# Chunked attention followed by a top-2 expert layer on one Trainium2 core: constants issued ahead of the loads, logits and rank products one iteration later, block-diagonal V and memory rows, selection by counting, and the spill one-hot in a pool of its own

## The chip, the cores and the metric

The kernel runs on one core of a Trainium2 chip. A core has five engines with a queue of instructions each: TensorE (PE, and PEld for its weight loads), VectorE (DVE), ScalarE (ACT), GpSimd (POOL) and SyncE (SP). The last two also issue DMA transfers here, as does ACT. The metric is the device time of one execution in microseconds (us), lower is better.

## What is computed

The reference has two stages. Attention works on chunks of 32 queries, each of which sees 16 keys to the left, its own 32, 8 to the right, and 8 memory keys (64 columns in all). Its output, 3072 rows of 512, goes through a router that picks two of eight experts for each row.

```python
# q, k, v: (4, 8, 768, 64); mem_k, mem_v: (4, 8, 8, 64); chunk, left, right = 32, 16, 8
for c in range(S // chunk):
    k_full = concat([mem_k, k[max(0, 32*c-16) : min(S, 32*c+40)]])
    v_full = concat([mem_v, v[...same rows...]])
    a = softmax(q[32*c : 32*c+32] @ k_full.T / 8)
    out[32*c : 32*c+32] = a @ v_full
x = out.transpose(0, 2, 1, 3).reshape(3072, 512)

noisy = x @ w_gate + log1p(exp(x @ w_noise)) * noise      # (3072, 8)
top2 = two largest of noisy per row;  w = softmax over those two
for e in range(8):
    for each row with e among its two:
        out[row] += w[row, e] * (relu(x[row] @ w1[e]) @ w2[e])   # w1 512x1024, w2 1024x512
```

## The kernel before

**Attention, 16 iterations.** The 32 heads are taken two at a time; such a pair fills the 128 partitions (head 0 on 0 to 63, head 1 on 64 to 127). Two pairs make a group, so there are eight groups of loads. All loads of Q, K, V and expert weights are issued by POOL in program order, which also issues the gathers and scatters later. `qg`, `kg` and `vg` have three buffers each; before the loop POOL issues groups 0, 1 and 2, and in the loop group `i // 2 + 2` at every even `i`.

The loop at L456 is a software pipeline, written out by hand; the order in the code is the order on every engine. Iteration `i` emits:

- `PT_pe(i-1)`: six PE transposes of the softmax numerators `P` into `p_p` (L259)
- `max_dve(i)`: DVE row maximum of the scores (L245)
- `qkT_pe(i+2)`: 24 PE transposes of Q and K into `p_t` (L212), with four ACT copies out of PSUM (L214)
- `PT_dve(i-1)`: DVE copy of `p_p` to `PT` (L264)
- `sub_dve(i)`: DVE subtraction of the maximum (L250) and ACT exponential to `P` (L252)
- `PV_pe(i-1)`: `PT` times memory rows and V into `ps_o` (L275, L281)
- `scores_pe(i+1)`: 116 small PE products into `ps_s`, of which there is one buffer (L224 to L237)
- `mult_dve(i-1)`: DVE reciprocal and scaling of `ps_o` into `xrow` (L292, L293)
- `xT_pe(i-2)`: six PE transposes of `xrow` into `p_x` (L301), and an ACT copy to `xt` (L303)
- `logits_pe(i-2)`: six PE products of `xt` with the gate and noise weights into `ps_l` (L311)

The PSUM tiles `p_p`, `p_t`, `p_x`, `ps_r` and `ps_t` share three buffers.

**Routing.** After every fourth pair a batch of 768 rows has its logits, and `route(b)` gives nine closures: `s1` (ACT softplus, DVE noisy logits `nl`), `s2` and `s3` (two rounds of maximum, comparison, code and maximum on DVE for the two experts `e1`, `e2`; from these the two-hot `two` and the pair one-hot `oh`; then PE rank products `ps_r`, L366 to L371), `s4` (gate weights, and an SP DMA of the rows to `x_rows`), `s4b` and `s5` (DVE token codes, ranks, and six one-hots `Rn`), `s6` (PE table `ps_t`, L407), `s7`, `s8` (DVE table `tab` and counts `seen`). The loop runs `s1` in the iteration that emits the batch's last logits and takes three closures from the list at the end of each iteration.

**Between the stages.** From the table the kernel forms the gather indices `gidx`, and from rows that overflow a bucket a spill list: `ov`, PE counts `ps_v`, the one-hot `sone` (DVE, L530), and its products `ps_w` (PE, L535). `sone` is in the pool `ap`, whose memory is given free after that; the gather buffers `xl` are laid over it.

**Experts.** POOL gathers 28 buckets of 128 rows by index (L572), PE transposes them (L581), and for eight experts PE does `ps_h` (L636) and `ps_y` (L644); DVE sums, POOL scatters (L652).

## Time and profile before

| | |
|---|---|
| median of 3 runs (lowest to highest) | 413.27 us (412.27 to 416.29) |
| the profiled execution: its time | 414.79 us |
| its span, first to last instruction | 413.1 us |
| PE busy | 307.4 us (74%), 4522 matmul instructions |
| DVE / ACT / POOL busy | 164.1 / 119.4 / 124.2 us |
| mean granted TensorE clock | 0.835 of 2.4 GHz |
| DMA | 42.98 MB, mean 104 GB/s |

The profile is one execution on the chip. A slice is a fortieth of the span, 10.3 us; slices 0 to 15 hold attention, and the experts' first product starts at 175.43 us. A matmul's recorded time includes its latency, so groups of matmuls are read from start to start.

### The profile page before, as it was taken

The numbers are of one execution on the slowest core, as the hardware profiler recorded it, in microseconds if no ns is written. First come the engines' busy times: TensorE is split into PE (matmuls) and PEld (weight loads), VectorE is DVE, ScalarE is ACT, GpSimd is POOL, SyncE is SP. The second block draws the span as 40 slices with busy tenths as digits, with TensorE's granted clock in tenths as the row PEclk, the third lists the DMA queues.
The fourth block names the chain that finished last, engine by engine and source line by source line (L and its number), as shares of the span: only waits on it lengthen the run. The fifth ranks groups of instructions, "written<-read, shape, count | busy, mean of one in ns | idle before, by whom it ended". The sixth has DMA issues, their size and how long they took to land.

```text
span 413.1 us, 10205 instructions
## 1 busy us (share of the span) xinstructions
PE 307.4 (74%) x4522; PEld 189.5 (46%) x4540; DVE 164.1 (40%) x377; ACT 119.4 (29%) x235; POOL 124.2 (30%) x141
## 2 busy tenths in 40 slices
PE   0045863766577462387899899899998999999990
PEld 0034652545456352264447447445454454554540
DVE  0005554745765776433214223233334242443440
ACT  1035643336335222022233233223130321312200
POOL 8840531315160000476110051060242403123061
PEclk9998585558556555578999999999999999999996
DMA  9999799699499520169960049068095852712021
GB/s 100 168 160 103 51 119 125 104 124 76 113 143 210 140 64 21 41 109 198 196 116 2 2 82 198 2 127 163 33 177 128 143 116 86 120 46 89 2 109 55
DMA packets 83327, 42.98 MB, mean 104 GB/s; under 512 B 57255, under 2 KB 76711, under 8 KB 83280
## 3 DMA queue, kind: packets, MB, share of 16 engines
q0 software_dynamic: 74928, 38.85, 65.1%
q1 hardware_dynamic: 8064, 3.38, 3.0%
q8 instruction: 37, 0.61, 0.6%
q10 hardware_dynamic: 288, 0.07, 0.1%
q14 instruction: 10, 0.08, 0.1%
HBM read 61.32 MB, written 10.65 MB: 174 GB/s over the span
## 4 chain that ended last, share of the span: by engine, by line
PE 65%; DVE 10%; issue 10%; ACT 5%; DMA 5%; POOL 3%; POOLq 0%; DVEq 0%; ACTq 0%
PE ps_h L636 23%; PE ps_y L644 20%; PE p_t L212 5%; DMA vg<-in_v_dram 4%; ACT xt L303 3%; PE p_x L301 2%; PE ps_o L281 2%; PE p_t L581 2%; PE p_p L259 2%; PE ps_o L275 2%; PE ps_s L234 2%; ACT qT L214 2%; POOL out_dram L652 2%; DVE xTb L582 1%; PE ps_l L311 1%
## 5 line engine op out<-in xcount | busy, mean ns | idle before, releaser
L636 PE MATMUL ps_h<-xTb,w1t 128*128 128x512 bf16 (+3 forms) x608 | 109.4, 330 | 1.1 <-DVE xTb L582 1.0
L644 PE MATMUL ps_y<-w2t,ht 128*128 128x512 bf16 x430 | 98.9, 379 | 1.0 <-issue 0.2
L636 PEld LDWEIGHTS <-w1t 128*128 128x128 bf16 x864 | 65.2, 99 | 46.0 <-issue 2.8
L624 DVE TENSOR_SCALAR ht<-ps_h 128x416 bf16<-128x416 f32 (+2 forms) x68 | 41.7, 613 | 82.9 <-PE ps_h L636 80.9
L652 POOL DMA_INDIRECT out_dram<-acc,sidx x28 | 28.0, 999 | 144.9 <-DVE acc L651 142.4
L644 PEld LDWEIGHTS <-ht 128*128 128x128 bf16 x448 | 42.3, 98 | 48.9
L622 ACT ACTIVATE ht<-ps_h 128x416 bf16<-128x416 f32 (+2 forms) x68 | 36.4, 535 | 80.8 <-PE ps_h L636 75.6
L117 POOL DMA_DIRECT2D vg<-in_v_dram x34 | 33.0, 975 | 61.0 <-PE ps_o L281 58.3
L572 POOL DMA_INDIRECT xl<-x_rows,gidx x28 | 29.2, 1041 | 68.2 <-DVE ov1b L515 46.6
L636 PE MATMUL ps_h<-xTs,w1t 128*128 128x32 bf16 x256 | 45.9, 179 | 0.2 <-issue 0.2
L648 ACT ACTIVATE acc<-ps_y,meta 128x512 f32<-128x512 f32 x28 | 19.2, 687 | 76.5 <-PE ps_y L644 43.1
L651 DVE SCALAR_TENSOR_TENSOR acc<-ps_y,meta,acc 128x512 f32<-128x512 f32 x28 | 21.0, 751 | 38.6 <-PE ps_y L644 38.6
L214 ACT CAST qT<-p_t 128x384 bf16<-128x384 f32 x32 | 17.2, 593 | 30.7 <-PE p_t L212 30.7
L582 DVE COPY xTb<-p_t 128x512 bf16<-128x512 bf16 x28 | 11.8, 423 | 28.8 <-PE p_t L581 28.5
L195 PE MATMUL p_m<-ident,mk_nat 32*128 32x32 f32 x4 | 0.6, 294 | 26.6 <-DVE ident L186 26.6
L303 ACT COPY xt<-p_x 128x768 bf16<-128x768 bf16 x16 | 12.8, 799 | 23.4 <-PE p_x L301 23.4
L581 PE MATMUL p_t<-identb,xl 128*128 128x128 bf16 x112 | 11.2, 225 | 10.9 <-DVE xTb L582 6.6
L212 PE MATMUL p_t<-identb,kg 128*64 128x128 bf16 x192 | 15.1, 285 | 4.2 <-ACT qT L214 3.7
L214 ACT CAST kT<-p_t 128x384 bf16<-128x384 f32 x32 | 17.5, 610 | 2.1 <-PE p_t L212 2.1
L245 DVE TENSOR_REDUCE mx<-ps_s 128x12 f32<-128x768 f32 x16 | 15.2, 951 | 7.2 <-PE ps_s L237 7.2
L252 ACT ACTIVATE P<-sd 128x768 bf16<-128x768 f32 x16 | 13.8, 863 | 8.1 <-DVE sd L250 8.1
L311 PE MATMUL ps_l<-wgn,xt 128*128 128x16 bf16 x96 | 5.2, 176 | 14.7 <-ACT xt L303 14.7
(130 smaller groups left out, 309.5 us busy)
## 6 DMA issues: line engine op xcount, KB each, us to landing
w1t<-in_moe_w_dram POOLq DMA_DIRECT2D x8, 1024.0 KB
w2t<-in_moe_w_dram POOLq DMA_DIRECT2D x8, 1024.0 KB
vg<-in_v_dram POOLq DMA_DIRECT2D x30, 168.0 KB
x_rows<-xrow SPq DMA_DIRECT2D x3, 792.0 KB, 5.1
qg<-in_q_dram POOLq DMA_DIRECT2D x6, 384.0 KB
kg<-in_k_dram POOLq DMA_DIRECT2D x6, 384.0 KB
qg<-in_q_dram POOLq DMA_DIRECT2D x4, 192.0 KB
kg<-in_k_dram POOLq DMA_DIRECT2D x4, 192.0 KB
```

The source lines that it names most:

```text
L117: nc.gpsimd.dma_start(out=vg[p0 + j:p0 + j + nj, x, c:c + n, :], in_=bass.AP(v.tensor, v.offset + (hd * S + c * chunk + j - left_ctx) * D, ...
L212: nc.tensor.matmul(out=p_t[64 * hh:64 * hh + 64, j, :], lhsT=src[:, 2 * i + hh, (SH * x + j) * D:(SH * x + j + 1) * D], rhs=identb, start= ...
L214: nc.scalar.copy(dst[:, :, SH * x:SH * (x + 1)], p_t.rearrange("d j p -> d p j"))
L303: nc.scalar.copy(xt, p_x)
L572: nc.gpsimd.indirect_dma_start(out=xl, out_offset=None, in_=xd, in_offset=bass.IndirectOffsetOnAxis(ap=gidx[:, p:p + 1], axis=0), bounds_c ...
L581: nc.tensor.transpose(out=p_t[:, kp, :], in_=xl[:, kp * 64:(kp + 1) * 64].bitcast(BF16), identity=identb)
L622: nc.scalar.activation(out=dst, in_=src, func=Act.Relu)
L624: nc.vector.tensor_scalar(out=dst, in0=src, scalar1=0.0, scalar2=None, op0=Alu.max)
L636: nc.tensor.matmul(out=ps_h[:, o:o + w], lhsT=w1t[:, kp, f * 128:(f + 1) * 128], rhs=rhs(kp), start=(kp == 0 and i == 0), stop=(kp == KP - ...
L644: nc.tensor.matmul(out=ps_y, lhsT=ht[:, f, j * CAP:(j + 1) * CAP], rhs=w2t[:, f, :], start=(f == 0), stop=(f == FB - 1))
L651: nc.vector.scalar_tensor_tensor(out=a, in0=ps_y, scalar=gate, in1=a, op0=Alu.mult, op1=Alu.add)
L652: nc.gpsimd.indirect_dma_start(out=out_part[p], out_offset=bass.IndirectOffsetOnAxis(ap=sidx[:, p:p + 1], axis=0), in_=a, in_offset=None, ...
```

## The change

- **Constants.** `upper`, the integer ramps and a new tile `tie` are made on POOL right after the first three V loads instead of after all loads of three groups. `ident`, which the very first PE work reads, is the first DVE cast instead of the last. `code` is gone. `scores_pe(0)` stands ahead of `qkT_pe(1)`.
- **V and memory rows block-diagonal.** Each V buffer now has a place for both heads side by side, zero where row and head don't match: 128 partitions x 6144 bf16. Three fixed buffers are cleared once by DVE ahead of everything; `memv` likewise. PV is then 6 products of 128 x 132 columns and 24 of 32 x 128 columns for a pair, with all 128 rows, instead of 12 of 65 and 48 of 64 columns with half the rows. The load of memory rows stands ahead of the second half of V of group 0.
- **Logits later.** `logits_pe(i-3)` stands behind `PT_pe(i-1)` at the head of an iteration, and the loop has one more iteration.
- **Routing.** `s2` selects by counting: differences of all pairs of the eight logits (6 x 64 per partition), a comparison with `tie`, a sum, and `< 2`. The rank products are in the step after. One step is taken for each iteration: (`s1`), (`s1b`, `s2`), (`s3`, `s4`), (`s4b`, `s5`), (`s6`), (`s7`, `s8`, together with the next).
- **Spill one-hot.** `sone` moves to the pool `rp`, which isn't given free.

```diff
+        vbufs = [ap_.tile([128, GP, ncnk, 2, D], BF16, name=f"vg{i}", bufs=1) for i in range(3)]
-            vg = ap_.tile([128, GP, ncnk, D], BF16, name="vg", bufs=3)
+        for vb in vbufs:
+            nc.vector.memset(vb, 0.0)
         new_group(0)
         load_qk(0, 0)
         ...
         load_v(0, 0)
+        upper = ...; ramp_i = ...; part_i = ...; tile_i = ...; tie = ...
...
         for c in range(ncnk):
             u, r = divmod(c, 4)
-            for hh in range(2):
-                hs = slice(64 * hh, 64 * hh + WIN)
-                nc.tensor.matmul(out=po[32 * r:32 * r + 32, hh, u * OW:u * OW + D], lhsT=PT[hs, u, 32 * r:32 * r + 32],
-                                 rhs=vg[hs, i, c, :], start=False, stop=True, skip_group_check=True)
+            nc.tensor.matmul(out=pv[32 * r:32 * r + 32, u // UB, u % UB, :, :D], lhsT=PT[:, u, 32 * r:32 * r + 32],
+                             rhs=vg[:, i, c], start=False, stop=True, skip_group_check=True)
...
+                nc.vector.tensor_tensor(out=df, in0=<nl over e>, in1=<nl over f>, op=Alu.subtract)
+                nc.vector.tensor_tensor(out=bt, in0=df, in1=tie, op=Alu.is_gt)
+                nc.vector.tensor_reduce(out=over, in_=bt, axis=AX, op=Alu.add)
+                nc.vector.tensor_scalar(out=two, in0=over, scalar1=2.0, scalar2=None, op0=Alu.is_lt)
...
-            return s1, s2, s3, s4, s4b, s5, s6, s7, s8
+            return (0, (s1,)), (0, (s1b, s2)), (0, (s3, s4)), (0, (s4b, s5)), (0, (s6,)), (1, (s7, s8))
...
-        for i in range(NPAIR + 2):
+        for i in range(NPAIR + 3):
             if 0 <= i - 1 < NPAIR:
                 PT_pe(i - 1)
+            if 0 <= i - 3 < NPAIR:
+                logits_pe(i - 3)
+                if (i - 3) % HP == HP - 1:
+                    begin, *rest = route((i - 3) // HP)
+                    begin[1][0]()
+                    pending.extend(rest)
             ...
             if 0 <= i - 2 < NPAIR:
                 xT_pe(i - 2)
-                logits_pe(i - 2)
-                if (i - 2) % HP == HP - 1:
-                    pending.extend(route((i - 2) // HP))
-                    steps(1)
             ...
             if i < NPAIR:
-                steps(3)
+                steps(1)
...
-        sone = ap_.tile([128, NP, SPILL], BF16, name="sone", bufs=1)
+        sone = rp.tile([128, NP, SPILL], BF16, name="sone")
```

On DVE, at the program's start (`vg`, `memv` are the V and memory tiles, `ramp_i` an integer ramp that POOL writes, `ident` the identity of the first transposes). Before:

```order
L123 MEMSET vg 32x32
L148 MEMSET memv 128x528
L149 MEMSET memv 128x16
L163 MEMSET onesb 128x128
L165 MEMSET neg 128x16
L172 CAST ramp<-ramp_i 128x128
...
L184 CAST wgn<-wgn_f 128x64
L186 CAST ident<-identb 32x32
```

With the change:

```order
L130 MEMSET vg0_88 128x3072
L130 MEMSET vg1_89 128x3072
L130 MEMSET vg2_90 128x3072
L160 MEMSET memv_128 128x1056
L162 MEMSET memv_128 64x16 [waits DVE_49]
L162 MEMSET memv_128 64x16
L178 CAST ident_154<-identb_98 32x32 [waits Pool_49]
```

The cast to `ident` no longer stands behind the cast of `ramp_i`, but behind four large clears.

On POOL, in the loads ahead of the loop (`qg`, `kg`, `vg` are loads of Q, K, V, `memv` those of memory rows; a DVE wait is one for DVE's clears). Before, from the second K load of group 0, and the end of group 2:

```order
L108 DMA kg_89<-in_k_dram 128x2x384
L117 DMA vg_90<-in_v_dram 56x24x64
L117 DMA vg_90<-in_v_dram 56x24x64 [waits DMASW0_49]
L151 DMA memv_116<-in_mem_v_dram 8x16x64 [waits DMASW1_49,DVE_49]
...
L108 DMA qg_121<-in_q_dram 128x4x384 [waits DMASW3_49]
...
L117 DMA vg_132<-in_v_dram 56x24x64 [waits DMASW6_49]
L167 MEMSET upper_143 128x128
...
L170 IOTA ramp_i_146 128x128
```

With the change, from V of pair 0 on:

```order
L118 DMA vg0_88<-in_v_dram 56x24x64
L137 MEMSET upper_106 128x128
...
L140 IOTA ramp_i_109 128x128
...
L109 DMA kg_95<-in_k_dram 128x2x384
L165 DMA memv_128<-in_mem_v_dram 8x16x64 [waits DVE_49]
...
L118 DMA vg0_88<-in_v_dram 56x24x64 [waits DMASW1_49]
L118 DMA vg0_88<-in_v_dram 56x24x64 [waits DMASW2_49]
L109 DMA qg_138<-in_q_dram 128x4x384 [waits DMASW3_49]
```

The integer ramp moved from behind all loads of three groups to behind the first five; the load of memory rows, which waits for DVE's clears, now has V of pair 1 and all of group 1 behind it.

On DVE, in the iteration that ends the first batch (`xrow` is the attention output, `nl` the noisy logits, `m`, `eq`, `c`, `e` the maximum, comparison, code and one-hot of one expert, `oh` the pair one-hot, `ge` and `gs` the gates, `ps_s` the scores). Before, with the two rounds of selection left out:

```order
L293 TENSOR_TENSOR xrow<-ps_o,rec 128x2x6x64
L330 TENSOR_TENSOR nl<-ns,nz_all 128x48
L331 TENSOR_TENSOR nl<-nl,ps_l 128x48
...
L356 TENSOR_TENSOR two<-e_1393,e_1408 128x96
L361 TENSOR_TENSOR oh<-two 128x192
L377 TENSOR_TENSOR ge<-ge,two 128x48
...
L380 TENSOR_TENSOR xrow<-ge,gs 128x6x8
L245 TENSOR_REDUCE mx<-ps_s 128x12
```

With the change:

```order
L294 TENSOR_TENSOR xrow<-ps_o,rec 128x6x128
L335 TENSOR_TENSOR nl<-ns,nz_all 128x48
L336 TENSOR_TENSOR nl<-nl,ps_l 128x48
L343 TENSOR_TENSOR df<-nl 128x384
L345 TENSOR_TENSOR bt<-df,tie 128x384
L347 TENSOR_REDUCE over<-bt 128x48
L349 TENSOR_SCALAR two<-over 128x96
L355 TENSOR_TENSOR oh<-two 128x192
L359 TENSOR_REDUCE m_1417<-nl 128x6
L361 TENSOR_TENSOR gd<-nl,m_1417 128x48
L251 TENSOR_REDUCE mx<-ps_s 128x12
```

Nine routing instructions stand between `xrow` and the next maximum `mx`; before, there were twenty (from `nl` to the gate weights in `xrow`), and PE's rank products stood in the same iteration as them.

## Rows read from the trace of the kernel before

**Rows 1.** The page: its span and the granted clock in 40 slices

```profile
span 413.1 us, 10205 instructions
PEclk9998585558556555578999999999999999999996
```

**Rows 2.** Timeline of the start: start us, us, engine, line, op, out<-in, count [idle before <-releaser]

```profile
1.03 0.50 DVE L148 MEMSET memv<- 128x528 uint32 x1
25.87 0.24 DVE L172 CAST ramp<-ramp_i 128x128 bf16<-128x128 int32 x1 [24.01 <-POOL ramp_i L170]
26.33 0.16 DVE L186 CAST ident<-identb 32x32 f32<-32x32 bf16 x1
26.55 0.63 PE L195 MATMUL p_m<-ident,mk_nat 32*128 32x32 f32 x4 [26.55 <-DVE ident L186]
```

**Rows 3.** Windows of 10 us: stretch, us, busy by engine, PEclk, DMA share, GB/s

```profile
0.00:10.00 10.00, 0.00 (x0) 0.00 (x0) 0.80 (x5) 1.28 (x1) 8.78 (x16) 1.00 1.18 98
10.00:20.00 10.00, 0.00 (x0) 0.00 (x0) 0.00 (x0) 0.00 (x0) 8.42 (x11) 1.00 1.77 169
20.00:30.00 10.00, 3.40 (x46) 2.86 (x47) 0.62 (x6) 2.58 (x7) 4.35 (x9) 1.00 2.02 160
```

**Rows 4.** Timeline of PE: six transposes into p_p at the heads of iterations

```profile
34.46 0.51 PE L259 MATMUL p_p<-identb,P 128*128 128x128 bf16 x6
41.07 0.82 PE L259 MATMUL p_p<-identb,P 128*128 128x128 bf16 x6
47.69 0.80 PE L259 MATMUL p_p<-identb,P 128*128 128x128 bf16 x6
60.37 0.80 PE L259 MATMUL p_p<-identb,P 128*128 128x128 bf16 x6
73.87 0.80 PE L259 MATMUL p_p<-identb,P 128*128 128x128 bf16 x6
...
151.56 0.80 PE L259 MATMUL p_p<-identb,P 128*128 128x128 bf16 x6
```

**Rows 5.** Waits of PE, 26 to 172 us: waiter <- waited for: us, times, longest

```profile
PE ps_l L311 <- ACT xt L303: 14.7, 16, 0.9
PE ps_r L366 <- DVE oh L361: 13.1, 3, 4.4
PE ps_s L234 <- issue: 3.6, 2, 2.1
```

**Rows 6.** Windows of one iteration each, at low and at high clock

```profile
41.00:47.70 6.70, 5.39 (x175) 4.27 (x172) 4.34 (x6) 3.58 (x6) 2.08 (x3) 0.50 0.07 7
51.20:57.90 6.70, 4.06 (x180) 3.18 (x178) 3.57 (x6) 3.88 (x7) 0.00 (x0) 0.99 1.38 151
```

**Rows 7.** Timeline of PE: PV of one pair, and products of 32 x 128 columns

```profile
44.01 0.51 PE L275 MATMUL ps_o<-memv,PT 64*128 64x65 bf16 x12
44.45 0.61 PE L281 MATMUL ps_o<-vg,PT 56*32 56x64 bf16 x48
44.99 0.32 PE L224 MATMUL ps_s<-mkT,qT 64*128 64x8 bf16 x12
...
202.89 0.63 PE L663 MATMUL ps_s<-w2t,ht 128*32 128x128 bf16 x32
```

**Rows 8.** Timeline from the last routing to the first expert product

```profile
162.07 0.27 DVE L361 TENSOR_TENSOR oh<-two 128x192 bf16<-128x192 bf16 x1
163.50 0.32 DVE L389 TENSOR_TENSOR rk<-oh,ps_r 128x168 f32<-128x168 bf16 x1
166.88 1.16 POOL L572 DMA_INDIRECT xl<-x_rows,gidx  x1 [46.63 <-DVE ov1b L515]
168.69 0.95 DVE L530 TENSOR_TENSOR sone<-ramp,srank 128x768 bf16<-128x768 bf16 x1
...
171.44 1.04 POOL L572 DMA_INDIRECT xl<-x_rows,gidx  x1 [3.40 <-PE p_t L581]
175.43 6.35 PE L636 MATMUL ps_h<-xTb,w1t 128*128 128x256 bf16 x32 [0.52 <-DVE xTb L582]
```

More of the change, by code (lines that the diff above doesn't have):

```diff
@@ L159, in body @@
         load_v(2)
+        ident = ap_.tile([32, 32], F32, name="ident", bufs=1)
+        nc.vector.tensor_copy(ident, identb[:32, :32])
         onesb = const.tile([128, 128], BF16, name="onesb")
@@ L328, in s1, with s1b @@
                 nc.scalar.activation(out=ns, in_=ns, func=Act.Ln, bias=1.0)
+                R["ns"] = ns
+            def s1b():
+                ns, ps_l = R["ns"], logits[b]
                 nl = T("nl", [128, BT, E])
@@ L449, in steps @@
             for _ in range(k):
-                if pending:
-                    pending.pop(0)()
+                while pending:
+                    late, fns = pending.pop(0)
+                    for fn in fns:
+                        fn()
+                    if not late:
+                        break
         qkT_pe(0)
+        scores_pe(0)
         qkT_pe(1)
-        scores_pe(0)
-        for i in range(NPAIR + 2):
+        for i in range(NPAIR + 3):
             if 0 <= i - 1 < NPAIR:
                 PT_pe(i - 1)
+            if 0 <= i - 3 < NPAIR:
[4 more added lines that the diff above has]
+                    pending.extend(rest)
             if i < NPAIR:
```

100 lines of the change are left out of this document (47 added, 53 removed).

## Prediction

> **What bounds the kernel now.** I read the page first. Its clock row [rows 1] parts the span: slices 16 to 39, the experts, run at a granted clock of 0.9 or more with PE nearly full, and nothing of the change touches their code. Slices 0 to 15, attention and routing, run mostly at 0.5, which is the 1.2 GHz level. So the change lives in the first 175.4 us, and I assume that from the first expert product on [rows 8] the remaining 413.1 - 175.4 = 237.7 us stay.
>
> In the first part I read four things. The timeline of the start [rows 2]: PE does nothing until 26.55, since its first product waits for `ident`, and `ident` stands on DVE behind a cast that waits 24.01 us for an integer ramp which POOL makes after issuing three groups of loads. The waits of PE [rows 5]: 14.7 us in 16 equal pieces (0.92 each) for ACT's copy `xt`, just ahead of the logits; 13.1 us in three pieces for the one-hot `oh`. The iteration heads [rows 4]: an undisturbed iteration at low clock takes 6.6 (41.07 to 47.69), one with routing 13.5 (60.37 to 73.87). From 41.07 (pair 1) to 151.56 (pair 15) there are 14 iterations; at 6.6 they would take 92.4, and they take 110.5, so routing, issue stalls and the short last iteration come to 18 net. Last the seam [rows 8]: the first gather is issued at 166.88, the second only at 171.44, after the spill products have read `sone`.
>
> **The change part by part.**
>
> *Start.* DVE now clears 3 x 3072 words and 1056 words ahead of `ident`. 528 words took 0.50 [rows 2], so the clears cost at most 3 x 2.9 + 1.0 = 9.7, and from 0.9 on `ident` is ready at about 11. PE starts at 11 instead of 26.55. But the loads don't come sooner. By the windows [rows 3] 1.0 MB had moved by 10 us, 2.7 by 20, 4.3 by 30. Pair 2's transposes, which stand ahead of pair 1's scores and of pair 0's exponential, need 2.3 MB: everything up to Q and K of group 1, before there at 17.8. Now POOL stops at the memory rows until DVE's clears end (near 10.6), with V of pair 1 and all of group 1 behind them; I give this 2 us. So PE pauses after pair 1's transposes until 20, and the first `p_p` comes at about 23 (I give the transposes, their copies and the exponential 3 us behind the landing, just under half an iteration) instead of 34.46. The head of the next iteration then stands at 29.5 instead of 41.07: 11.6 gained. Bounds: 7 if group 1 comes 5 us later than before, 15.5 if nothing waits. Group 2's Q and K (3.8 MB, before at 27, now 29) are wanted at 30, so they are just hidden.
>
> *Logits later.* `xt` is copied while the next `p_p` transposes (0.80) run, so the 0.92 goes, in all 14 iterations. At the end of the loop two such waits stay.
>
> *Block-diagonal PV.* Before, 12 products take 0.44 and 48 take 0.54 from start to start at low clock [rows 7]: 0.98 a pair. Now 6 of 132 columns; the nearest row is `p_p`, 6 of 128 in 0.80 with 0.31 latency, so 0.7. And 24 products of 128 rows x 32 with 128 columns. The experts have this very shape: 32 of them take 0.63 at high clock [rows 7], next start 0.56 later, 17 ns each; 24 are 0.4 at high clock and at most twice that at low, I take 0.63. Sum 1.33, 0.35 more than before, at low clock; at high clock, where the new form halves and the old one was bound by issue in part, I take them as even. This is a loss, not a gain, unless the lower count of instructions (960 fewer rows on PE) cuts the issue stalls, of which one place shows 3.6 us in two pieces [rows 5]; of those I let 1.5 us remain on top of the iterations. Upper bound: no two of the 24 overlap, 0.1 each by the `p_p` row, 2.4 + 0.7 a pair.
>
> This is where a page speaks against the change. The Trainium skill, "TensorE: Matmul & The Clock Gate", Part 3, says that products with few rows should sit in different row groups, where they run concurrently, and that one with 32 rows takes as long alone as one with 128. By that the merged form gives up the row packing and the array's time doubles, which would make the sum that of a rival below, 387 (0.98 x 2, worked out there from rows). No row here shows a PV without row packing; that products on different column groups overlap, which the same part says, the expert stage's 17 ns for 128 columns bears out.
>
> *Clock.* At low clock an iteration is then 6.6 - 0.92 + 0.35 = 6.03, nearly all of it PE work (5.39 busy in the 6.7 shown [rows 6], plus 0.35). At high clock PE was busy 4.06 and ACT 3.88 of an iteration [rows 6]; with one waiting for the other now and then I take 4.6. The clock rose in before only after stretches without a gap, and fell after them; with the `xt` gap gone I let it be high in four iterations of ten: 0.6 x 6.03 + 0.4 x 4.6 = 5.46. Bounds 6.03 and 4.6. 14 x 5.46 = 76.4, less 2.4 since the last iteration has no transposes and scores.
>
> *Routing.* PE no longer stands before `oh`, since the rank products come a step later. But DVE does the selection in one piece between `xrow` and the next maximum. Three instructions of 384 elements, 0.55 each (between 168 in 0.32 and 768 in 0.95 [rows 8]), and six small ones of 0.2 to 0.27: 3.0 us, where DVE has 3.57 of its own each iteration [rows 6]. From the end of a PV to the next PV, DVE then needs 1.2 (scaling: 768 elements in 0.95 and a small one) + 3.0 + 0.95 (maximum, 768 elements) + 0.55 (`PT`, by what 3.57 leaves beside three of 0.95 and a small one) = 5.7, PE 4.7 at low clock, 4.0 at high: a stall of 1.0 to 1.7. The exponential of the gates, on ACT ahead of the next transposes' copies, ends within the same stall. The step with the six `Rn` (ten instructions of 0.2 to 0.32, 2.2 us) costs 0.5, the rank and table products on PE 1.4, and `ps_r` and `ps_t` keep one of the three shared PSUM buffers for two iterations, 0.7. About 4.2 for a batch, 2.6 batches in the loop: 11. Nothing of before is left of the 13.1.
>
> *Seam.* The gather still waits for its table. Ahead of it stand the remaining steps of batch 2 (ten DVE instructions of the same kind and the table, some 3.5 us, against 3 of transposing, copying and logits on the other engines), and PV's 0.35: from pair 15's `p_p` to the first gather 16.8 instead of 166.88 - 151.56 = 15.3. The selection itself is shorter by some 0.5, in that sum. Then `sone` no longer holds the second gather: before 175.43 - 166.88 = 8.55 from the first gather to the first product, now 5.5: the second gather is issued 1.4 behind the first (1.16 and a gap), and the product comes 4.0 behind it as now (171.44 to 175.43). Together 22.3 instead of 23.87.
>
> **Sum.** Pair 15's `p_p` at 29.5 + 76.4 - 2.4 + 11 + 1.5 = 116.0 instead of 151.56. Plus 22.3 and 237.7: a span of 376.0. The profiled execution took 414.79 at a span of 413.1, 1.7 more, and the median shown, 413.27, is 1.5 lower than it. So 376.2; I say **376**.
>
> **The rivals.**
>
> *PE stays at 1.2 GHz.* Low clock was the rule in these slices [rows 1], and the transposes that fill PE are the same. Then 14 x 0.57 = 8 more: 384. 22 in 100. Its mirror, high clock throughout (14 x 0.86 = 12 less), 364: 10 in 100.
>
> *The loads or DVE become the bound.* A group is 1.5 MB, 9 us at 160 to 170 GB/s, for two iterations of 5.5: little slack, and each V load waits for a PV two iterations back. Or the selection delays PE by twice what I have. Either costs 8 to 10: 385. 13 in 100.
>
> *PV costs twice what it did.* Twice the columns pass through the array without row packing: 0.98 x 2, against 1.33 in the sum, 0.65 x 16 = 10.5 more: 387. This is the skill's rule of above. The expert stage's row [rows 7] is for it only at low clock, where 24 products would need 0.8 and not 0.63. 5 in 100.
>
> *PV is slower still, and the kernel slower than before.* If the 24 products neither overlap nor hide their loads of 128 rows, each takes 0.2 at low clock, the six likewise: 6.0 a pair instead of 1.33, 4.7 x 16 = 75 more, so 451. It decides from a PV of 3.6 us a pair, where 2.3 x 16 eat the gain of 37; mere lack of overlap (3.1) gives 404. Against it stands the row of the expert stage with this shape. 6 in 100, a little over half of it above 417.
>
> *The early constants don't bring PE forward,* because data holds it until where it was: pair 2's Q and K landing at 31 instead of 20 would give 387. The windows of the start [rows 3] speak against it. 4 in 100.
>
> **How the numbers follow.** The forecast with its own spread, 368 to 382: 40 in 100. The cases together leave under 2 in 10 outside 362 to 393, which I give as the range. A difference of 1% (4 us) is about what can be told from no change here. Faster 0.94, same 0.02, slower 0.04: only the slow PV reaches the last two.
>
> **What would show it.** First PE work near 11, first `p_p` near 23, with a wait of PE for a transfer or an idle stretch between; no wait of PE for `xt` but at the end; PV of about 1.3 from start to start at low clock; no wait for `oh`, but waits for `PT` in the iterations with the selection; pair 15's `p_p` near 116; gathers 1.3 apart; the first `ps_h` 22 behind it. I am wrong if the iterations don't come to 5 to 6 us, above all through the clock, or if the part behind the first `ps_h` doesn't keep its 237.7.

## The result and the profile after

The changed kernel took **394.6 us** (median of four executions, 393.64 to 396.0) beside 413.14 for the kernel before: a ratio of 0.9547, 95% interval 0.9495 to 0.9599. Faster, as forecast, but by 18.5 us instead of 37, and outside the range by 1.6. The profiled span is 393.1 where the sum said 376.0. Medians here are over all executions; e4_mem_late, e6_wlate and e9_ge_later each have one slow execution among their four, and without it they come to 383.78, 395.52 and 388.17. Here is the sum beside that trace, section by section:

| section | before | predicted | after | miss |
|---|---|---|---|---|
| start to pair 1's `p_p` | 41.07 | 29.5 | 32.75 | +3.3 |
| 14 iterations, pair 1's `p_p` to pair 15's | 110.5 | 86.5 | 95.4 | +8.9 |
| pair 15's `p_p` to the first gather | 15.3 | 16.8 | 15.8 | -1.0 |
| first gather to the first `ps_h` | 8.55 | 5.5 | 13.8 | +8.3 |
| first `ps_h` to the end | 237.7 | 237.7 | 235.4 | -2.3 |

So the error lies in the loop and in the seam, about half in each; the start's is cancelled by two small ones the other way.

The page of after, answering to [rows 1]: span, and the granted clock in 40 slices.

```profile
span 393.1 us, 9217 instructions
PEclk9999555898885655699999999999999999999997
```

The timeline of PE at the start, answering to [rows 2]:

```profile
12.27 0.63 PE L199 MATMUL p_m<-ident,mk_nat 32*128 32x32 f32 x4 [12.27 <-DVE ident L178]
...
22.74 0.85 PE L216 MATMUL p_t<-identb,qg 128*64 128x128 bf16 x12 [5.06 <-DMA qg<-in_q_dram]
25.11 0.85 PE L216 MATMUL p_t<-identb,kg 128*64 128x128 bf16 x12 [1.52 <-DMA kg<-in_k_dram]
...
27.48 0.82 PE L265 MATMUL p_p<-identb,P 128*128 128x128 bf16 x6 [0.71 <-ACT P L258]
```

POOL's queue in the same stretch shows what held the loads: a wait of 0.82 for the first clear, 1.37 us of constants (7.08 to 8.45) that now stand ahead of loads, and 2.04 for the last clear.

```profile
4.43 2.66 POOL L118 DMA_DIRECT2D vg<-in_v_dram  x3 [0.82 <-DVE vg L130]
7.08 0.22 POOL L137 MEMSET upper<- 128x128 bf16 x1
...
8.45 0.75 POOL L109 DMA_DIRECT2D qg<-in_q_dram  x1
9.19 0.73 POOL L109 DMA_DIRECT2D kg<-in_k_dram  x1
11.96 1.29 POOL L165 DMA_DIRECT2D memv<-in_mem_v_dram  x2 [2.04 <-DVE memv L160]
```

So the second 10 us moved 105 GB/s where [rows 3] has 169 (window row: stretch, us, busy by engine, clock, DMA share, GB/s):

```profile
10.00:20.00 10.00, 4.75 (x116) 3.97 (x116) 4.25 (x13) 4.15 (x9) 8.04 (x10) 1.00 1.15 105
```

The waits of PE over the 14 iterations, 32.75 to 128.12, answering to [rows 5] (waiter <- waited for: us, times, longest):

```profile
PE ps_o L279 <- DVE PT L270: 8.9, 4, 4.2
PE p_t L216 <- ACT qT L218: 7.3, 7, 3.0
PE ps_l L313 <- ACT xt L305: 3.8, 10, 0.6
PE p_t L216 <- issue: 3.6, 2, 2.5
PE p_t L216 <- DVE PT L270: 1.5, 3, 0.7
PE p_x L303 <- issue: 1.3, 1, 1.3
PE p_p L265 <- issue: 1.2, 1, 1.2
```

No wait for `oh` is left in the loop, and the one for `xt` fell to 3.8. Over the same iterations of before it was 12.8:

```profile
PE ps_l L311 <- ACT xt L303: 12.8, 14, 0.9
```

PV of one pair at low clock, answering to [rows 7]: 0.77 and 0.76 from start to start.

```profile
64.00 0.84 PE L279 MATMUL ps_o<-memv,PT 128*128 128x132 bf16 x6
64.77 0.83 PE L282 MATMUL ps_o<-vg,PT 128*32 128x128 bf16 x24
65.53 0.32 PE L230 MATMUL ps_s<-mkT,qT 64*128 64x8 bf16 x12
```

The seam, answering to [rows 8]: the second gather stands 1.46 behind the first, but the 96 spill products, which took 0.92 before, run in ten pieces until 154.5.

```profile
143.89 1.16 POOL L580 DMA_INDIRECT xl<-x_rows,gidx  x1 [48.42 <-DVE ov1b L523]
145.35 1.04 POOL L580 DMA_INDIRECT xl<-x_rows,gidx  x1 [0.30 <-issue]
...
146.70 0.43 PE L543 MATMUL ps_w<-ovc,sone 128*32 128x2 bf16 x37 [2.42 <-issue]
147.51 0.21 PE L543 MATMUL ps_w<-ovc,sone 128*32 128x2 bf16 x3 [0.37 <-issue]
148.24 0.23 PE L543 MATMUL ps_w<-ovc,sone 128*32 128x2 bf16 x5 [0.52 <-issue]
...
154.11 0.44 PE L543 MATMUL ps_w<-ovc,sone 128*32 128x2 bf16 x32 [0.56 <-issue]
```

### The profile page after: what moved, and what is told of

It reads as the page before. It is cut to its first block, busy times and chain, and to the rows that moved or that the text cites. A ratio compares the mean times of both kernels' runs of the same rounds, so it can differ in the third digit from the quotient of the medians.

```text
span 393.1 us, 9217 instructions
## 1 busy us (share of the span) xinstructions
PE 304.5 (77%) x4042; PEld 188.6 (48%) x4060; DVE 169.9 (43%) x350; ACT 119.8 (30%) x235; POOL 124.5 (32%) x143
## 4 chain that ended last, share of the span: by engine, by line
PE 60%; DVE 15%; issue 10%; DMA 7%; ACT 3%; POOL 3%; POOLq 0%; DVEq 0%; ACTq 0%
PE ps_h L644 24%; PE ps_y L652 21%; DMA x_rows<-xrow 4%; PE p_t L216 3%; DMA kg<-in_k_dram 2%; PE ps_o L279 2%; PE ps_o L282 2%; DVE xrow L294 2%; PE p_t L589 2%; DVE vg L130 2%; DVE xTb L590 2%; POOL out_dram L660 2%; DVE mx L251 1%; ACT qT L218 1%; PE p_x L303 1%
## 5 line engine op out<-in xcount | busy, mean ns | idle before, releaser
L644 PE MATMUL ps_h<-xTb,w1t 128*128 128x512 bf16 (+3 forms) x608 | 107.8, 328 | 1.1 <-DVE xTb L590 1.0
L216 PE MATMUL p_t<-identb,kg 128*64 128x128 bf16 x192 | 14.1, 275 | 10.5 <-ACT qT L218 7.7
L251 DVE TENSOR_REDUCE mx<-ps_s 128x12 f32<-128x768 f32 x16 | 15.2, 950 | 12.1 <-PE ps_s L243 12.1
L305 ACT COPY xt<-p_x 128x768 bf16<-128x768 bf16 x16 | 12.8, 799 | 22.5 <-PE p_x L303 22.5
L216 PE MATMUL p_t<-identb,qg 128*64 128x128 bf16 x192 | 11.5, 265 | 9.5 <-DMA qg<-in_q_dram 5.1
L279 PE MATMUL ps_o<-memv,PT 128*128 128x132 bf16 x96 | 11.2, 273 | 9.4 <-DVE PT L270 9.4
L294 DVE TENSOR_TENSOR xrow<-ps_o,rec 128x768 bf16<-128x768 f32 x16 | 15.3, 958 | 5.3 <-DMA x_rows<-xrow 4.8
```

The costliest lines, as they stand in the source:

```text
L216: nc.tensor.matmul(out=p_t[64 * hh:64 * hh + 64, j, :], lhsT=src[:, 2 * i + hh, (SH * x + j) * D:(SH * x + j + 1) * D], rhs=identb, start= ...
L294: nc.vector.tensor_tensor(out=xr, in0=po.rearrange("p x (u h) c -> p x u h c", h=2)[:, :, :, :, :D], in1=rec.rearrange("p x (u h o) -> p x ...
L644: nc.tensor.matmul(out=ps_h[:, o:o + w], lhsT=w1t[:, kp, f * 128:(f + 1) * 128], rhs=rhs(kp), start=(kp == 0 and i == 0), stop=(kp == KP - ...
```

## Experiments on the seam: the pieces

**e1_sone_back** makes `sone` in the attention pool again.

```diff
-        sone = rp.tile([128, NP, SPILL], BF16, name="sone")
+        sone = ap_.tile([128, NP, SPILL], BF16, name="sone", bufs=1)
```

> The changed kernel with one line undone: the spill one-hot sone is again made in the attention pool, so that the second gather waits for the spill products as before. Theory A (the indirect gathers that POOL now issues back to back slow down PE's instruction supply, and that is why the 96 spill products take 7.8 us in pieces): with one gather in flight the products take about 0.9 us again, the first expert product comes 8.5 us behind the first gather instead of 13.8, and the kernel is about 5 us faster than the changed one (389 to 390). Rival B (the pieces come from where these 96 instructions lie in the program, gathers or not): the products stay at 7 to 8 us, the second gather starts only behind them, and the kernel is 2 to 4 us slower than the changed one (397 to 399).

Measured 394.79 (ratio 0.9591, 0.9532 to 0.9651). The edit did not bring back the state it was to bring back: the gathers stood at 142.04 and 143.50, the second as little held as after the change. Probably `sone`, with the larger buffers of the changed kernel, no longer lies where the second gather writes; the trace does not show places in memory. The pieces were there, 13.8 again. It decides nothing between A and B. It does show that the line on `sone` by itself does nothing in this layout.

**e2_psw24** sums the spill in 24 products and spreads the rows with one more.

```diff
-            for j in range(4):
-                nc.tensor.matmul(out=ps_w[32 * j:32 * j + 32, :], lhsT=sone[:, t, :], rhs=ovc[:, t, :], ...)
+            nc.tensor.matmul(out=ps_q, lhsT=sone[:, t, :], rhs=ovc[:, t, :], ...)
+        nc.vector.tensor_copy(sq, ps_q)
+        nc.tensor.matmul(out=ps_w, lhsT=rep.rearrange("p o r -> p (o r)"), rhs=sq, start=True, stop=True)
```

> The changed kernel with the spill products in a quarter of the instructions: 24 products into 32 rows, a copy to SBUF and one product with a repeated identity that spreads the rows, in place of 96. Theory A (PE's instructions are supplied slowly while gathers run): the 24 products still come in pieces, about a quarter of them, 2 us instead of 7.8, the first expert product 8 us behind the first gather, the kernel about 5 us faster (389 to 390). Rival B (each spill product is slow for its own sake, by its operands): the 24 take 7.8 / 4 = 2 us evenly spread, not in pieces. Rival C (the wait is for something else that ends at 154, not for instructions): the products or what follows them still end 10 us behind the first gather, and the kernel stays at 394 to 395.

Measured 390.92 (0.9471, 0.9415 to 0.9526). The 24 products take 0.80 by PE's records, but DVE's copy of them begins only at 148.53, 3.7 behind their end, and the first `ps_h` comes 12.1 behind the first gather. So a quarter of the products bought 1.7 us and not 5 at this place, which is nearest to C, while the kernel's time is the one that A gave (389 to 390). The cause is not their number alone.

**e10_spill_late** moves the spill products and their gather behind the first 32 expert products.

```diff
                     first(W1[e], ht, off, ps, x == 2)
+                    if x == 0:
+                        s_gi, s_si = spill_index()
+                        gather_spill(s_gi)
```

> The changed kernel with the 96 spill products, their index and the spill gather moved behind the first two transposes and the first 32 expert products. Theory A: nothing of the spill stands between the gathers and the first expert product, so that comes 5.5 us behind the first gather as the prediction had it (13.8 now); the spill products, now with no gathers in flight, take about 0.9 us, and the kernel is about 7 us faster than the changed one (387 to 388). Rival C (PE would have waited for the gathered rows anyway, since the transfers are slow with several in flight): the first transposes wait for xl and start at 154 as now; gain under 2 us.

Measured 391.0 (0.9502, 0.9436 to 0.9569), 4 to 5 us less than the two variants beside it that show the pieces (e1, and e6 below). The first `ps_h` stands 5.5 behind the first gather (141.96 to 147.46), as in the prediction, and the moved products take 0.90 in one run. C falls: the gathered rows were there. Not all of the 8.3 us gained at this place stays: from the first `ps_h` to the end it takes 238.8, where e1 and e6 take 235.8 and 235.5.

Four variants on another chip (e3, e4, e5 and e9, below) had no pieces, though e3 and e4 leave PE's products as they are. So the changed kernel itself was run again, three times, each on a different chip.

> The changed kernel itself once more, as a measure for the runs beside it. In its first trace and in three of its variants on one chip the spill products took 7 us and more in pieces; in four other variants on another chip, two of which leave PE's program as it is, they took 1.02 without a pause. Theory K (the pieces depend on the chip or on how the program was loaded, not on the code): here too they can be whole, then the first expert product comes 6.3 us behind the first gather and the kernel takes 386 to 390. Theory A (the code with its back-to-back gathers brings them wherever it runs): 13.8 us behind the gather and 393 to 396.

> The changed kernel itself a third time, as the measure for the three runs beside it. Theory K (the pieces of the spill products depend on the chip or the loading): either outcome is possible here, 385 to 388 with the products whole and the first expert product 6.3 us behind the first gather, or 393 to 396 with pieces and 13.8; nothing between. Against it: a value between, or pieces that come and go between runs on one chip (times 8 us apart within this run).

> The changed kernel a fourth time, as the measure for the run beside it: 385 to 388 with the spill products whole (the run beside it then tells nothing new), or 394 to 397 with them in pieces.

Measured 386.25 (0.9395, 0.9346 to 0.9444), 396.68 (0.9596, 0.9544 to 0.9649) and 386.02 (0.9418, 0.9380 to 0.9455). The first and the third have the products whole, the second in pieces; no execution lies between. The timeline of PE in r1_again:

```profile
145.33 1.02 PE L543 MATMUL ps_w<-ovc,sone 128*32 128x2 bf16 x96 [1.45 <-DVE sone L538]
...
149.78 5.97 PE L644 MATMUL ps_h<-xTb,w1t 128*128 128x256 bf16 x32 [0.52 <-DVE xTb L590]
```

and in r2_again:

```profile
149.59 0.43 PE L543 MATMUL ps_w<-ovc,sone 128*32 128x2 bf16 x37 [2.38 <-DVE sone L538]
150.33 0.23 PE L543 MATMUL ps_w<-ovc,sone 128*32 128x2 bf16 x3 [0.31 <-issue]
...
160.44 5.78 PE L644 MATMUL ps_h<-xTb,w1t 128*128 128x256 bf16 x32 [0.52 <-DVE xTb L590]
```

Theory K stands: the same program has a first `ps_h` 6.3 behind the first gather (143.48 to 149.78) on some chips and 13.6 to 13.8 on others, 7.5 us that belong to where it runs or how it was loaded. The kernel before has its 96 products whole in the one trace of it (0.92), yet it too is slower beside the runs with pieces, 412.65 to 413.14 against 409.8 to 410.92; so 2 to 3 of the 8 to 10 us between the changed kernel's runs need not be the pieces. In both kinds one block of instructions is fetched just as the gathers start, by the DMA view of 144 to 145 in r1_again and in after, in this order:

```profile
q8 instruction: 1, 0.02, 7.6%
```

```profile
q8 instruction: 1, 0.02, 7.7%
```

So the fetch alone does not make the pieces. **e11_gather_hold** lets only the first gather start ahead of the spill gather; it was run twice.

```diff
-        for p in plan[0]:
-            gather(p)
+        gather(plan[0][0])
         gather_spill()
+        for p in plan[0][1:]:
+            gather(p)
```

> The changed kernel with the spill gather put second on POOL's queue, so that all gathers but the first wait until the spill products are done, about as before. Theory A (several gathers in flight slow PE's instruction supply): the spill products take about 0.9 us in one piece, the first expert product comes 9 to 10 us behind the first gather, the kernel is 3 to 4 us faster than the changed one on a chip where that shows pieces. On a chip where the changed one shows none, this one is 3 us slower than it (the second gather comes 3 us later). Rival B (the pieces come from the place of the products in the program, where a new block of instructions begins): they stay, and the kernel is 2 to 4 us slower than the changed one.

> The kernel of e11_gather_hold once more: all gathers but the first wait until the spill products are done. On a chip where r3_again shows pieces: by theory A (the gathers in flight are needed for the pieces) the products take 0.9 in one run, the first expert product stands 9.4 us behind the first gather, and the kernel takes about 391, 4 us less than r3_again; by rival B (the new block of instructions alone brings them) the pieces stay and the kernel takes 397 or more. On a chip without pieces it takes 4 us more than r3_again, as on the earlier chip (390.7 against 386.3).

Measured 390.67 (0.9515, 0.9465 to 0.9565) beside r1_again's 386.25, and 391.23 (0.9575, 0.9521 to 0.9629) beside r3_again's 386.02. Both times the chip was one without pieces, so A and B stay untested against each other. What the pair does show is the price of holding the second gather: the first `ps_h` 9.4 behind the first gather instead of 6.3, 4 to 5 us in all. The 3.1 at this place is the gain that the prediction put down to `sone`.

## Experiments on the start

**e4_mem_late** puts the two loads of the memory rows behind V of pair 1 and Q and K of group 1 (the block moves down three lines).

> The changed kernel with the loads of the memory rows put behind V of pair 1 and Q and K of group 1 on POOL's queue, so that POOL no longer stands until 11.96 for DVE's clears. Theory G (the hold of POOL costs what it lasts): Q of pair 2 lands about 2 us earlier than 22.7, PE's waits for qg and kg shrink, the first p_p comes at 25 to 26 instead of 27.5, the kernel 1.5 to 2.5 us faster (392 to 393). Rival H (the DMA engines were full with what had been issued before, so the hold costs nothing): Q of pair 2 lands within 0.5 us of now, no gain.

Measured 384.01 (0.9380, 0.9318 to 0.9442). Theory G holds at its place: K of pair 2 lands 2.7 earlier and the first `p_p` comes 2.7 earlier than in after, and the kernel is some 2 us under the repeats without pieces. PE's timeline:

```profile
22.37 0.85 PE L216 MATMUL p_t<-identb,kg 128*64 128x128 bf16 x12 [2.48 <-DMA kg<-in_k_dram]
24.74 0.82 PE L265 MATMUL p_p<-identb,P 128*128 128x128 bf16 x6 [0.72 <-ACT P L258]
```

**e8_before_ident** is the kernel before with one move, `ident` ahead of the constants.

> The kernel before with one move alone: the small identity ident is made ahead of the constants that wait for POOL, so PE's first product waits for neither ramp nor clears; V's layout, the loads' order and all else stay. Theory N (without the clears, data alone sets the start): PE starts at 3 to 9, Q and K of group 1 land at about 18 as before the change, the first p_p comes at 22 to 25 instead of 34.5, and the kernel is 8 to 11 us faster than before (402 to 405). Rival (other constants behind the ramp, such as wgn for the logits, hold PE until 27 anyway): the first p_p at 25 to 27 but the first logits wait, gain 5 to 8 us. In either case the difference of the first p_p to the changed kernel's 27.5 is the price of the clears and the hold on POOL.

Measured 406.23 (0.9897, 0.9864 to 0.9929): the rival. K of pair 2 is there at 21.23, nearly 4 us before the changed kernel, but the maximum of pair 0 stands on DVE behind the ramp cast until 26, and PE waits for it:

```profile
21.23 0.85 PE L212 MATMUL p_t<-identb,kg 128*64 128x128 bf16 x12 [2.08 <-DMA kg<-in_k_dram]
28.09 0.32 PE L224 MATMUL ps_s<-mkT,qT 64*128 64x8 bf16 x12 [6.01 <-DVE sd L250]
28.97 0.82 PE L259 MATMUL p_p<-identb,P 128*128 128x128 bf16 x6
```

So `ident` alone buys 5.5 us at the first `p_p` (28.97 for 34.46) and 4.7 in all. The changed kernel's first `p_p` is 1.5 earlier still, with the integer constants ahead of the loads; a later place for DVE's casts, which might do the same without holding the loads, was not run. In the changed kernel K of pair 2 came 3.9 later than here, for 0.82 + 1.37 + 2.04 = 4.2 of holds on POOL's queue; e4, which takes the last of them away, is left with 1.1 (22.37 against 21.23).

## Experiments on the loop

**e6_wlate** asks for the first weights two iterations later (13 instead of 11).

> The changed kernel with the first expert weights' loads issued two iterations later (13 instead of 11). Theory D (pair 12's scaled rows wait 4.0 us on DVE because batch 1's row write, 14.1 us instead of 4.5, stands behind the weights on the DMA engines, and its buffer is wanted again): the write lands in 4 to 6 us, the wait of xrow is gone, the wait of PV for PT at 117 falls from 4.2 to under 1, and the kernel is 3 to 4 us faster (390 to 392). Rival E (DVE is late there anyway, for its own work on the routing): the wait goes but the heads stay within 1 us, and the kernel stays at 394.

Measured 395.88 (0.9571, 0.9488 to 0.9654), with pieces. The edit moved nothing: the weights were issued at 93.46 (93.03 in after), because no instruction on POOL's queue ahead of them waits for the later iteration. It tells nothing on D.

**e3_xrow3** gives `xrow` a third buffer (`bufs=2` to `bufs=3`).

> The changed kernel with three buffers for xrow instead of two. Theory D (pair 12's scaling waits 4.0 us on DVE because it wants the buffer whose row write, issued at 101 just behind three weight loads, takes 14.1 us to land): the wait of xrow for the write is gone, the wait of PV for PT at 117 falls from 4.2 to under 1, pair 15's head comes 3 to 4 us earlier against pair 1's head, and the kernel is 3 to 4 us faster (390 to 392). Rival E (DVE is late there anyway for its routing work): the wait goes, the heads keep their distance within 1 us, no gain.

Measured 386.57 (0.9405, 0.9366 to 0.9444), no different from the repeats without pieces, 386.25 and 386.02. In after, DVE waits for the row write, which with the weights on the DMA engines takes up to 14.1 us to land:

```profile
110.78 0.23 DVE L293 RECIPROCAL rec<-ps_o 128x12 f32<-128x12 f32 x1 [0.68 <-PE ps_o L282]
115.03 0.96 DVE L294 TENSOR_TENSOR xrow<-ps_o,rec 128x768 bf16<-128x768 f32 x1 [4.02 <-DMA x_rows<-xrow]
```

With three buffers that wait is gone, the two iterations around it are 1.2 shorter than in r1_again (12.84 and 14.05), and the loop as a whole is 95.5 against 95.1. D is right on the wait and wrong on its price, as far as single traces can tell: the same loop takes from 93.5 (e1) to 98.8 (r2_again).

**e9_ge_later** moves the gates' exponential on ACT an iteration later.

```diff
+                R["gd"] = gd
+            def s3():
                 R["ge"] = T("ge", [128, BT, E])
-                nc.scalar.activation(out=R["ge"], in_=gd, func=Act.Exp)
-            def s3():
+                nc.scalar.activation(out=R["ge"], in_=R["gd"], func=Act.Exp)
```

> The changed kernel with the gates' exponential on ACT moved from the selection to the next step, an iteration later. Theory F (in the selection's iterations ACT stands up to 3.3 us before that exponential, with the copies of the next Q and K transposes queued behind it, and PE waits 2.1 and 3.0 us for them): PE's long waits for qT at 71 and 96 fall under 1 us, the two iterations get 1.5 to 3 us shorter each, the kernel 3 to 5 us faster (390 to 392). Rival (DVE is the bound of those iterations: the scores' maximum and PT stand behind the selection on DVE, so PE waits for PT instead): the waits for qT turn into waits for PT and the two iterations lose less than 1 us each.

Measured 388.86 (0.9452, 0.9392 to 0.9513), no gain on the repeats: the rival. The wait for `qT` of 3.0 became 0.5, and a wait of PV for `PT` of 2.27 stands in its place; the iteration takes 9.17 (9.23 in r1_again). DVE's selection is what ends last there, as the prediction had it.

**e7_no_loads** leaves out the loads of groups 3 to 7.

```diff
-                new_group(g)
...
+                groups[g] = groups[g % 3]
```

> The changed kernel without the loads of Q, K and V of groups 3 to 7: their pairs compute on the rows of groups 0 to 2, so that from about 45 us on the DMA engines carry only the three weight loads, row writes and instructions. Theory L (PE's issue stalls in the loop, 6.2 us between 37 and 61, come from instruction fetches that stand behind the loads on full DMA engines): the stalls after 45 are gone (3.6 of 6.2), and with more clock the 14 iterations get 4 to 7 us shorter. Rival M (they come with so many instructions, whatever else moves): the same stalls at the same instructions. Batch 1's row write, still behind the weights, shows what the weights alone do to it: with theory D the wait of xrow stays 3 to 4 us.

Measured 378.79 (0.9223, 0.9177 to 0.9270), 7.5 less than r1_again. Its loop takes **85.8 us, where the prediction said 86.5**. The window of the 14 iterations in e7, then in after, then in r1_again (stretch, us, busy PE, PEld, DVE, ACT, POOL, clock, DMA share, GB/s):

```profile
32.05:117.82 85.77, 62.84 (x1841) 50.49 (x1831) 63.26 (x132) 47.83 (x85) 1.01 (x2) 0.91 0.43 68
```

```profile
32.75:128.12 95.37, 66.15 (x1840) 53.07 (x1831) 63.71 (x132) 47.70 (x85) 30.29 (x34) 0.74 1.34 137
```

```profile
32.27:127.34 95.07, 65.92 (x1841) 52.94 (x1831) 63.71 (x132) 47.69 (x85) 30.31 (x34) 0.80 1.34 137
```

PE's issue waits over the loop are 1.9 in e7, 6.3 in after, and 3.3, 8.1 and 7.0 in r1_again, r2_again and r3_again, whose loops take 95.1, 98.8 and 96.3. In after the four that last over 1 us (of 1.1 to 2.5) each end 1.4 to 1.9 us behind the landing of a block of instructions, so theory L is right on what PE stands for. But these waits are not the larger part: of the 9.3 us between r1_again and e7, PE's busy time makes 3.1, its waits for `PT` 3.5 (9.3 against 5.8), the issue waits 1.4 and the waits for loads 0.9.

The clock in these rows needs care. The profile reads 1.00 until the first entry of its record of the clock, which stands at 51.1 in e7, while the transposes into `p_p` at 39.14 and 45.24 take 0.84, their time at low clock (0.49 to 0.52 at high). With the stretch ahead of that entry taken as low, the loop's mean is 0.80 in e7, 0.77 in r1_again and 0.73 in after.

The wait of `xrow` that D expected to stay did not: the weights, with no V loads ahead of them on POOL, had gone out earlier, and one wait of 0.8 at the end is left.

**e5_rowpacked** and **e13_rowpacked_no_loads** bring back the products of PV by heads, on the same block-diagonal buffers; e13 has e7's edit too.

```diff
-                nc.tensor.matmul(out=pv[:, u // UB, u % UB], lhsT=PT[:, u, :], rhs=memv[:, n], ...)
+                for hh in range(2):
+                    hs = slice(64 * hh, 64 * hh + 64)
+                    nc.tensor.matmul(out=po[:, hh, u * OW:u * OW + D + 1], lhsT=PT[hs, u, :], rhs=memv[hs, n, hh, :D + 1], ...)
```

> The changed kernel with the products of PV made as before, for each head by itself (12 of 65 columns and 48 of 64 columns, on 64 and 56 rows), from the same block-diagonal buffers with the same clears and loads; the scaling reads the old layout. Theory I (the merged form costs 1.53 a pair at low clock against 0.98 and is even at high clock): each low-clock iteration gets 0.5 us shorter, with half of them at low clock 3 to 4 us in all, unless the 30 more products a pair bring issue stalls. Rival J (PE's instruction supply is what runs short: 480 more products and their weight loads cost as many stalls as before): issue stalls grow by 2 us or more, and the kernel is no faster than the changed one (394 or over).

> The changed kernel without the loads of groups 3 to 7 (their pairs compute on the rows of groups 0 to 2) and with the row-packed products of PV of before. Theory J (row-packed PV lost 7 us under load because its 480 further products and their weight loads need more blocks of instructions, which come late on full DMA engines): with the DMA engines free the issue stalls after 45 are gone, the loop from pair 1's head to pair 15's is within 3 us of the 85.8 that merged PV takes without loads, and the kernel within 3 us of 378.8. Rival I' (row-packed is slow on PE or DVE for its own sake, in this order of work): the loop stays 5 to 7 us longer, 384 to 386.

e5 measured 393.01 (0.9554, 0.9507 to 0.9601) without pieces: 7 us **slower** than the changed kernel in its repeats without them, 1.4 to 1.7% by the ratios, and 4 to 6 slower than e3 and e9 on its own chip (386.57 and 388.86), though each PV takes less of PE's time (0.44 and 0.54 at low clock). Its window of the loop and its largest waits:

```profile
32.86:133.10 100.24, 70.97 (x2258) 58.80 (x2251) 63.76 (x131) 47.34 (x85) 30.16 (x34) 0.64 1.23 130
```

```profile
PE ps_s L240 <- issue: 11.3, 5, 3.7
...
PE ps_o L286 <- issue: 3.8, 3, 2.0
PE p_t L216 <- issue: 2.1, 3, 1.1
```

Issue waits come to 18.0, over 18 blocks of instructions where the merged form needs 15. Yet PE's waits in all are only 1.8 more than r1_again's (30.3 and 28.5); it is PE's busy time that is 5.1 longer, 70.97 against 65.92. e13 measured 390.66 (0.9481, 0.9429 to 0.9532), with pieces; its loop takes

```profile
33.06:122.02 88.96, 68.20 (x2259) 56.80 (x2252) 63.28 (x131) 47.38 (x85) 0.19 (x1) 0.83 0.39 63
```

3.2 more than e7's, with 8.6 of issue waits (1.9 in e7) and, in all, 21.6 of waits (22.2 in e7). J asked for a loop and a kernel within 3 us of e7's, I' for a loop 5 to 7 longer and 384 to 386; less some 7.5 for the pieces the kernel is at 383, an estimate, so neither is met. One iteration, from pair 5's `p_p` to pair 6's, shows the form without routing and without issue waits: merged in after, row-packed in e5, row-packed in e13.

```profile
60.90:66.94 6.04, 5.68 (x138) 4.64 (x137) 2.68 (x5) 3.89 (x8) 1.02 (x2) 0.50 1.01 75
```

```profile
63.98:69.48 5.50, 5.14 (x169) 4.34 (x168) 3.17 (x6) 3.88 (x8) 1.04 (x2) 0.50 0.62 44
```

```profile
60.62:66.11 5.49, 5.13 (x169) 4.34 (x168) 3.19 (x6) 3.89 (x8) 0.00 (x0) 1.00 0.03 7
```

The last two are alike to 0.01, so the 1.00 of e13, whose record of the clock begins at 75.0, is low clock too. At that clock the row-packed iteration is 0.54 **shorter**: theory I is right there. What stands against the form is how little of its loop runs at the high level: by the record, with the stretch ahead of its first entry taken as low, 10 us of 100 in e5 and 17 of 89 in e13, against 51 of 86 in e7, 44 of 95 in after and 34 to 55 in the other merged traces with loads. Whether the further issue waits or the products themselves keep the clock down is not shown.

## A better version

**b1_mem_spill** joins e4 and e10; **b2_mem_spill_xrow** adds e3's third buffer.

> Two edits together: the memory rows' loads behind group 1's Q and K (2.3 us in the earlier run by the first p_p), and the spill products behind the first 32 expert products (first expert product 5.5 us behind the first gather instead of 6.3, or instead of 13.8 where the products come in pieces). Theory: 2.5 to 3.5 us faster than the changed kernel on a chip without pieces (383 to 384), 8 to 10 us on one with them. Rival (the loop takes back what the start gives, since loads and not PE set the pace until 60): less than 1.5 us on a chip without pieces.

> As b1_mem_spill, with three buffers for xrow. Theory D (the wait of xrow for the row write behind the weights is on the path): 1 to 2 us faster than b1 (the two iterations around it were 1.2 us shorter in the earlier run with three buffers, in place of the 4 first expected). Rival E: within 1 us of b1.

Beside r2_again's 396.68, on a chip with pieces, b1 took 386.8 (0.9361, 0.9314 to 0.9408) and b2 **384.96** (0.9330, 0.9289 to 0.9372), 11.7 less than the changed kernel and 28 less than the kernel before there. The first `ps_h` stands 5.5 behind the first gather in both. b2 is 1.8 under b1, within both intervals, so the third buffer is not shown to be worth anything. Behind the first `ps_h` they take 240.0 and 238.7, beside 236.7 in r2_again: as in e10, the moved products cost 2 to 3 us there. Where the products run whole the move has 0.8 to gain at the seam (6.3 to 5.5), so it may lose; it was not run on such a chip, where e4 alone took 384.01.

## Point by point

**Start: right in kind, short by 3.3.** PE started at 12.27 (11 said) and waited for data as said. Two steps failed. The first is "before there at 17.8", read off the bytes moved: in e8, whose loads stand in the order of before, K of group 1 is there at 21.23, when by [rows 3] some 2.9 MB had moved and not 2.3, so loads issued later had a share. The second is "POOL stops ... I give this 2 us". The stop was 2.04, but two more holds stand ahead of it on the same queue, 0.82 for the first clear and 1.37 for the moved constants; I had put the constants ahead of the loads without charging the loads for them. So K of pair 2 came at 25.11, not 20. From there to pair 1's `p_p` it took 7.6 (9.5 said), which hid 1.9 of the 5.1.

**Logits: nearly.** The wait for `xt` was to go from all 14 iterations; 3.8 of 12.8 is left, in ten pieces of 0.6 at most.

**Loop: the loads were not free, and the sum without them came out in part by luck.** Without loads the 86.5 came out at 85.8. But nine of e7's 14 iterations begin with transposes of 0.49 to 0.52, the high clock's, where the sum has 5.6 (four in ten); with nine, its own terms give 82 (5 x 6.03 + 9 x 4.6 - 2.4 + 11 + 1.5). Iterations without routing took 4.8 to 4.9 at high clock (4.6 said) and 6.1 to 6.3 at low (6.03), and the better clock made up for it. The step that failed is the cover: "just hidden" for the loads and 1.5 us for issue stalls. With them the loop costs 9 more: PE is busy longer at a lower clock, its issue waits are 3.3 to 8.1, and `xrow` waits 4.02 for a row write behind the weights, which the sum put at nothing. Two things were open to see. The rival on loads (385, 13 in 100) came near the 386 of the repeats without pieces, but not by its mechanism: PE waits for no load of Q, K or V in the loop of after, and for 0.8 to 2.5 us of them in the repeats. And [rows 5] shows only the issue waits of one product; over the loop of before there were two more lines:

```profile
PE ps_s L234 <- issue: 3.6, 2, 2.1
...
PE ps_o L281 <- issue: 2.8, 3, 1.6
PE p_p L259 <- issue: 2.0, 1, 2.0
```

8.4 in all, not 3.6. I had let the smaller count of instructions cut them to 1.5, though the same bytes are loaded in less time; they were 3.3 to 8.1.

**PV: priced a little low, right at equal clock, wrong for the kernel.** 1.53 a pair at low clock (1.33 said), 0.90 at high (0.44 and 0.46), against 0.98 at low clock and, in e13, 0.77 at high for the row-packed form. (The rival's 0.65 is 0.63 by its own terms, so its 387 is 386.) By Part 3 of the Trainium skill's page "TensorE: Matmul & The Clock Gate", small products in different row groups of the array run concurrently. The 1.53 that the merged form takes in place of 0.98 agrees in direction. So I called the edit a loss, and at equal clock it is one; yet the kernel with the old form is slower, with a loop that stays at low clock and has more issue waits. The prediction named the issue stalls as a reservation, and the clock not at all in this place.

**Clock: higher than said.** 44 of the 95 us of after's loop and 51 of r1_again's are at the high level; four iterations in ten, by the sum's terms a third of the time, were said. That the missing `xt` gap brings it is not borne out: e5, without the gap, has 10 us of 100, and e8, with it, 17 of 109. What goes with it is the products' form: the four traces with row-packed products (before, e8, e5, e13) have 10 to 17 us at the high level, all merged ones 34 to 55. By what way is open.

**Routing: right in size, a little low.** In e7, without other disturbance, the two iterations with the selection take 7.96 and 8.99 beside neighbours of 4.8 to 4.9, the ones with `Rn` 6.06: 4.3 to 5.3 a batch, 4.2 said. The stall shows first as PE's wait for `qT`, behind the exponential of the gates, and not for `PT`; e9 turns one into the other and gains nothing.

**Seam: right where the products run whole.** To the first gather 15.8 (16.8 said, though the terms named, 15.3 and 0.5 of DVE and 0.35 of PV, come to 16.2). From there to the first `ps_h` 6.3 without pieces (5.5 said): the step "the product comes 4.0 behind it as now" leaves out the 96 products, which stand between. On the chip of the result it was 13.8. These 7.5 no row of before shows, and the runs can't say what makes them. With r1_again's 386 the miss is 10 us: 2.8 at the start, 8.6 in the loop, 0.8 here, less 1.9 in the other two sections.

**Experts:** 235.2 to 236.7 in the traces that leave this part as it is, where 237.7 stood before. e8, whose code there is that of before, takes 235.8 too, so the 2 us are not the change's.

## What to carry to other kernels

Sum the issue waits of an engine over every line of a stretch, and ask what the DMA engines do meanwhile: here a loop that got faster with the same loads kept most of those waits. Price a merge of products at each level of the clock, and look at which level the loop then runs. Hold a granted clock of 1.00 at the start of a trace against the time of a group that repeats. Before a difference of 2% is explained from one trace, run the same kernel on another chip.

## What was not expected of the hardware

Blocks of instructions are transfers like others: the DMA view of the loop shows 15 of them, 0.25 MB, and where loads fill the DMA engines PE stands up to 3.7 us for one (59.39 to 63.12 in e5, with a block landing at 61.7). The Trainium skill, "Runtime: NRT & Kernel Launch", "Instruction fetch mechanics", describes these blocks of 16 KiB on a DMA queue of the sequencer's own and calls their cost mostly hidden; the sizes agree, but here the waits come to 1.9 us with few loads and to 18.0 at the most with them.

On some chips PE ran, in the middle of the 96, one to five small products in each 0.7 to 0.8 us while indirect gathers were in flight, on others all 96 in 1.02. Whether the gathers are needed for that stays open.

A DVE clear of 3072 words took 2.62, with 0.59 between one and the next.
